# Row sums on TensorE for five attention units: four matmuls of 128 queries in place of sixteen of 32

## The chip, the cores and the metric

The kernel runs on one core of a Trainium2 chip. The metric is the device time of one execution in microseconds. The kernel before took 599.05 us (median of 3 runs, 598.12 to 600.31).

## The reference: what is computed

Chunked attention, and behind it a feed-forward block with a rational activation:

```python
for c in range(nc):                       # 24 chunks of 32 queries, per batch (4) and head (8)
    q_c = q[:, :, c_start:c_end]
    k_full = np.concatenate([mem_k, k_ctx], axis=2)   # 8 + up to 56 keys
    v_full = np.concatenate([mem_v, v_ctx], axis=2)
    scores = scale * np.matmul(q_c, k_full.transpose(0, 1, 3, 2))
    a = np.exp(scores - np.max(scores, axis=-1, keepdims=True))
    a = a / (np.sum(a, axis=-1, keepdims=True) + 1e-09)
    out[:, :, c_start:c_end] = np.matmul(a, v_full)
...
h = x @ w_in                              # x: 3072 x 512, w_in: 512 x 2048
P = a[0] + a[1] * h + a[2] * h2 + a[3] * h3
Q = 1.0 + np.abs(b[0]) * np.abs(h) + np.abs(b[1]) * h2
return (P / (Q + 1e-06)) @ w_out          # w_out: 2048 x 512
```

The weights w_in and w_out come as 64-bit floats and are turned into pairs of 32-bit ones on the chip.

## The kernel before, in words

The 3,072 tokens are six blocks of 512. A block's attention is worked in four units (i, p), one for each pair of heads: i is the block, p the pair. A unit has 16 chunks of 32 queries, and 64 keys for each of the two heads.

An early unit (i of 0 or 1) goes through these steps, each a function named here with its lines:

- att_scores (354): 16 matmuls of 32 queries each, which fill a PSUM tile of 128 x 512; places (268) puts four chunks at the four quarters of the 128 partitions, with a tile position for each.
- att_max, att_less (364, 371) on VectorE, att_exp (394) on ScalarE, and for a sequence's ends memsets on GpSimd (absent, 381).
- att_turn (404): four transposes of 128 x 128 into a PSUM tile ep; att_keep (414): ScalarE copies it to the SBUF tile eT. There the 128 partitions are the keys of both heads, and the 512 columns are the queries, chunk after chunk.
- att_values (421): 16 matmuls, each with the 32 columns of eT of one chunk as the weights and that chunk's values (128 x 128) as the moving side (line 428). For the five units in SUMS_PE (line 36: (0,0), (0,2), (1,0), (1,1), (1,2)) it then adds 16 matmuls with the same weights against a matrix "ones" of two columns, one for each head (line 434). They write the row sums into the first 8 columns of ep, which is free by then.
- att_more (330) reads the sums from ep on VectorE (line 334) and att_over (340) inverts them. For the other early units att_sums (319) takes the sums on VectorE instead (line 324).
- att_norm (437) scales the values, att_back (446) transposes back, att_hi and att_lo (456, 463) split the result into two parts for the feed-forward block.

The feed-forward block: g1 (480, matmuls at 489) makes h for 128 of the 2,048 features, a chain of steps on ScalarE, VectorE and GpSimd (554 to 614; chain_mend at 602 is the last but two) makes the activation, and g2 (491, matmuls at 504) adds its product with w_out. Each product is three matmuls of 128 x 128 weights and 512 columns. 96 such rounds run over the six blocks.

Order: up to the 31st round the order is written out by hand in SEQ (line 50), a list of tokens that is worked through once (740); each engine keeps the program's order (pin, 141). A lower-case "d" is att_values, "D" is att_more, "G" is att_over, "n" att_norm, "b" att_scores, "m" and "M" att_max and att_less, "x" att_exp, "c" att_turn, "k" att_keep, "e" att_back; "f" and "g" are g1, "o" is g2, "W" is a warm-up transpose (663), "P" a small matmul that spreads six parameters over the partitions (732). Around the first unit it reads "... d00 D00 b03 v01 w x02 M01 q10 G00 n00 x01 m03 W c02 c01 M03 e00 A k02 B d02 z01 D02 ... W W d01 ...". The PSUM tiles of the early units come from pa (260), which goes round four rooms: the values' tile of (0,2) is the room of the scores of (0,3), and the values' tile of (0,1) is the room of ep of (0,2), where its sums lie.

Of the kernel before, what the change touches and what calls it, by code (L numbers as in the profile page):

```python
# [19 lines left out]
CHUNK = 32  # L20
# [69 lines left out]
def attn_moe(ctx, tc, qk, vm, w, ab, out, seq):  # L90
    nc = tc.nc
    P = 128
# [5 lines left out]
    NC, NG = TB // CHUNK, TB // P  # L98
# [30 lines left out]
    ones = const.tile([P, 2], F32, name="ones")  # L129
# [11 lines left out]
    def pin(ins):  # L141
        if pinned[0]:
            tc.keep_in_program_order(ins)
# [116 lines left out]
    def pa(i):  # L260
        turn[0] = (turn[0] + 1) % 4
        if early[0]:
            if turn[0] == 3:
                return ps_r.tile([P, 512], F32, name="pa", tag="cr")
            return ps_o.tile([P, DM], F32, name="pa", tag=f"o{turn[0]}")
        return ps_a.tile([P, 512], F32, name="pa", tag="pa")

    def places(i):
        return [(g, j, 4 * g + j if i < BLOCKWISE else NG * j + g) for g in range(NG) for j in range(4)]
# [40 lines left out]
    def pair_values(i, p):  # L310
        u = unit[i, p]
        ov = u["o"] = two_banks("o", D)
        for g, j, c in places(i):
            for h in range(2):
                pin(nc.tensor.matmul(ov[j * CHUNK:(j + 1) * CHUNK, h, g],  # L315
                                     lhsT=u["eT"][h * KEYS:(h + 1) * KEYS, c * CHUNK:(c + 1) * CHUNK], rhs=u["v"][c][h],
                                     start=True, stop=True, tile_position=(h * KEYS, j * CHUNK)))
# [103 lines left out]
    def att_values(i, p):  # L421
        if i >= BLOCKWISE:
            return pair_values(i, p)
        u = unit[i, p]
        o = u["o"] = pa(i)
        ov = o.rearrange("x (g h d) -> x g h d", g=NG, h=2)
        for g, j, c in places(i):
            pin(nc.tensor.matmul(ov[j * CHUNK:(j + 1) * CHUNK, g],  # L428
                                 lhsT=u["eT"][:, c * CHUNK:(c + 1) * CHUNK], rhs=u["v"][c],
                                 start=True, stop=True, tile_position=(0, j * CHUNK)))  # L430
        if (i, p) in SUMS_PE:
            sv = u["ep"][:, :2 * NG].rearrange("x (g h) -> x g h", h=2)
            for g, j, c in places(i):
                pin(nc.tensor.matmul(sv[j * CHUNK:(j + 1) * CHUNK, g], lhsT=u["eT"][:, c * CHUNK:(c + 1) * CHUNK], rhs=ones,  # L434
                                     start=True, stop=True, tile_position=(0, j * CHUNK)))

    def att_norm(i, p):
        if i >= BLOCKWISE:
# [182 lines left out]

    att = {}
    pieces = dict(z=att_sums, D=att_more, G=att_over, b=att_scores, m=att_max, M=att_less, x=att_exp, c=att_turn, k=att_keep, d=att_values, n=att_norm, e=att_back, h=att_hi, l=att_lo)

    def plan(n, kind, i, p):
# [218 lines left out]
```

## Time and profile before

| | |
|---|---|
| median of 3 runs | 599.05 us (598.12 to 600.31) |
| the profiled execution | 598.73 us |
| its span, first to last instruction | 596.9 us |
| mean granted TensorE clock | 1.000 |
| matmul records on TensorE | 5,111, and as many loads of weights |
| busy: TensorE, VectorE, GpSimd, ScalarE | 98%, 78%, 68%, 67% |

PE is TensorE's matmuls and PEld its loads of weights, DVE is VectorE, ACT ScalarE, POOL GpSimd, SP the queue that issues the DMAs. L434 is line 434 of the kernel. An entry "128*32 128x2" of PE stands for weights of 128 rows and 32 columns and a moving side of 2 columns. Matmuls are pipelined, so their records overlap and a line's busy time is less than its count times the mean. "issue" is time in which an engine waited for nothing that the profile shows.

### The profile page before, as it was taken

The page shows a single profiled execution, that of the slowest core. Times are in us where ns is not written, and L with a number is a line of the kernel's source. Part 1 is how long each engine was busy: PE and PEld are TensorE (multiplying, and loading weights), DVE is VectorE, ACT ScalarE, POOL GpSimd, SP SyncE. Part 2 cuts the span into 40 slices and gives each one's busy share as a digit, 9 for nine tenths or more (in the row PEclk, how much of TensorE's full clock was granted, in tenths as well). Part 3 has the DMA queues.
Part 4 walks back from the last instruction along what each step waited for, and adds up shares of the span by engine and source line. Part 5 has one row for each costly group of instructions (what it writes and reads, how often), then busy time and mean ns, then how long its engine had stood idle before and what let it go on. Part 6 is the DMA issues. An engine that isn't in the chain of part 4 may idle for free.

```text
span 596.9 us, 13088 instructions
## 1 busy us (share of the span) xinstructions
PE 586.8 (98%) x5111; PEld 478.4 (80%) x5111; DVE 464.9 (78%) x762; ACT 401.9 (67%) x665; POOL 406.4 (68%) x376
## 2 busy tenths in 40 slices
PE   7899999999999999999999999999999999999997
PEld 6677888888787878878888888888888888888886
DVE  5899999898797759888877778787787766666673
ACT  4699999898667655656566666565765656755673
POOL 5468998798546766576677576766667677667682
PEclk9999999999999999999999999999999999999999
DMA  8965346230345344332331422312510100100001
GB/s 304 406 206 213 146 177 212 72 128 13 124 131 165 98 151 127 94 111 72 99 87 50 154 43 87 94 36 81 178 36 1 37 10 9 71 1 1 0 1 70
DMA packets 34591, 61.14 MB, mean 102 GB/s; under 512 B 4066, under 2 KB 20706, under 8 KB 34146
## 3 DMA queue, kind: packets, MB, share of 16 engines
q1 hardware_dynamic: 34386, 60.18, 30.6%
q8 instruction: 40, 0.66, 0.5%
q14 instruction: 21, 0.17, 0.1%
q10 hardware_dynamic: 144, 0.13, 0.1%
HBM read 44.56 MB, written 7.34 MB: 87 GB/s over the span
## 4 chain that ended last, share of the span: by engine, by line
PE 95%; DVE 2%; ACT 1%; DMA 1%; issue 0%; SPq 0%; POOL 0%; DVEq 0%
PE h L489 44%; PE o L504 43%; PE pairs L315 2%; PE pairs L293 2%; PE pa L428 1%; PE pa L361 1%; DMA qk<-in_qk_dram 1%; PE pa L412 1%; PE pa L454 0%; DVE e L379 0%; PE pa L434 0%; ACT e L396 0%; DVE ct L602 0%; ACT eT L419 0%; PE warm L663 0%
## 5 line engine op out<-in xcount | busy, mean ns | idle before, releaser
L489 PE MATMUL h<-x_hi,w_hl 128*128 128x512 f32 x768 | 240.3, 394 | 0.4 <-DVE ct L602 0.3
L504 PE MATMUL o<-w_hl,ghi 128*128 128x512 f32 x768 | 236.8, 390 | 0.0
L566 POOL TENSOR_TENSOR cy<-cy,ha 128x512 f32<-128x512 f32 x96 | 124.6, 1298 | 140.4 <-ACT cy L562 135.8
L504 PEld LDWEIGHTS o<-w_hl,ghi 128*128 128x128 f32 x768 | 143.9, 188 | 29.8 <-ACT v_main L546 0.2
L489 PEld LDWEIGHTS h<-x_hi,w_hl 128*128 128x128 f32 x768 | 141.7, 188 | 32.4 <-DVE ct L602 1.1
L489 PE MATMUL h<-x_lo,w_hl 128*128 128x512 f32 x384 | 150.0, 391 | 0.2 <-POOL x_lo L467 0.2
L504 PE MATMUL o<-w_hl,glo 128*128 128x512 f32 x384 | 150.0, 391 | 0.0
L614 POOL TENSOR_TENSOR glo<-ct,ghi 128x512 fp32r<-128x512 f32 x95 | 122.9, 1294 | 9.1 <-ACT ghi L609 3.2
L594 DVE SCALAR_TENSOR_TENSOR ct<-ct,par,h 128x512 f32<-128x512 f32 x82 | 61.2, 746 | 56.2 <-ACT h L590 55.5
L575 DVE TENSOR_TENSOR ct<-ct,h 128x512 f32<-128x512 f32 x96 | 65.6, 684 | 39.4 <-ACT ct L571 37.8
L586 ACT ACTIVATE h<-cy 128x512 f32<-128x512 f32 x82 | 49.1, 599 | 69.5 <-DVE ct L579 56.1
L557 ACT ACTIVATE ha<-h 128x512 f32<-128x512 f32 x96 | 57.4, 598 | 54.4 <-PE h L489 54.3
L607 POOL TENSOR_TENSOR ghi<-ct,zero 128x512 fp32r<-128x512 f32 x81 | 84.2, 1040 | 2.5 <-PE o L504 1.2
L504 PEld LDWEIGHTS o<-w_hl,glo 128*128 128x128 f32 x384 | 72.1, 188 | 16.8 <-POOL glo L614 1.6
L489 PEld LDWEIGHTS h<-x_lo,w_hl 128*128 128x128 f32 x384 | 72.1, 188 | 16.1 <-POOL x_lo L467 0.6
L562 ACT ACTIVATE cy<-ha,bab 128x512 f32<-128x512 f32 x96 | 78.4, 817 | 2.6
L571 ACT ACTIVATE ct<-h,par 128x512 f32<-128x512 f32 x96 | 73.6, 766 | 5.6 <-PE h L489 5.5
L579 DVE SCALAR_TENSOR_TENSOR ct<-ct,par,h 128x512 f32<-128x512 f32 x96 | 71.6, 746 | 3.0
L602 DVE SCALAR_TENSOR_TENSOR ct<-h,ct 128x512 f32<-128x512 f32 x82 | 56.5, 689 | 2.6
L598 DVE SCALAR_TENSOR_TENSOR h<-cy,h 128x512 f32<-128x512 f32 x82 | 56.5, 689 | 0.0
L590 ACT ACTIVATE h<-h 128x512 f32<-128x512 f32 x82 | 47.7, 582 | 2.6
L204 POOL TENSOR_TENSOR w_hl<-w_raw,w_hl 128x512 fp32r<-128x512 f32 x32 | 42.0, 1318 | 6.4 <-ACT w_hl L199 5.7
(80 smaller groups left out, 461.9 us busy)
## 6 DMA issues: line engine op xcount, KB each, us to landing
w_raw<-in_w_dram SPq DMA_DIRECT2D x26, 512.0 KB, 5.9
qk_pairs<-in_qk_dram SPq DMA_DIRECT2D x16, 576.0 KB, 4.2
v_main<-in_vm_dram SPq DMA_DIRECT2D x16, 512.0 KB, 5.1
out_dram<-v_main SPq DMA_DIRECT2D x23, 256.0 KB, 2.3
qk<-in_qk_dram SPq DMA_DIRECT2D x16, 288.0 KB, 5.8
eT<-blocks SPq DMA_DIRECT2D x64, 64.0 KB, 2.1
xf<-blocks SPq DMA_DIRECT2D x64, 64.0 KB, 2.1
v_main<-in_vm_dram SPq DMA_DIRECT2D x12, 256.0 KB, 6.4
```

The source lines that it names most:

```text
L489: pin(nc.tensor.matmul(h, lhsT=wt[:, cols], rhs=xt[i][:, ct, :], start=ct == m == 0, stop=ct == NCT - 1 and m == 2))
L504: ins = nc.tensor.matmul(o, lhsT=gt[:, cols], rhs=wt, start=begin and m == 0, stop=end and m == 2)
L557: pin(nc.scalar.activation(c["ha"], c["h"], AF.Abs))
L562: pin(nc.scalar.activation(c["y"], c["ha"], AF.Identity, scale=B1, bias=B0))
L566: pin(nc.gpsimd.tensor_tensor(c["y"], c["y"], c.pop("ha"), op=ALU.mult))
L571: pin(nc.scalar.activation(c["t"], c["h"], AF.Identity, scale=A3, bias=A2))
L575: pin(nc.vector.tensor_tensor(t, t, h, op=ALU.mult))
L579: pin(nc.vector.scalar_tensor_tensor(t, t, A1, h, op0=ALU.add, op1=ALU.mult))
L594: pin(nc.vector.scalar_tensor_tensor(t, t, A0, r, op0=ALU.add, op1=ALU.mult))
L598: pin(nc.vector.scalar_tensor_tensor(r, yy, QC, r, op0=ALU.add, op1=ALU.mult))
L607: pin(nc.gpsimd.tensor_tensor(ghi, chain[z]["t"], zero.broadcast_to([P, TB]), op=ALU.add))
L614: pin(engine.tensor_tensor(glo, chain.pop(z)["t"], gh[z].bitcast(F32), op=ALU.subtract))
```

## The change

The loop over the 16 places becomes a loop over the four groups of 128 queries; a group's four chunks lie next to each other in eT, and their sums go to the same places in ep as before.

```diff
         if (i, p) in SUMS_PE:
             sv = u["ep"][:, :2 * NG].rearrange("x (g h) -> x g h", h=2)
-            for g, j, c in places(i):
-                pin(nc.tensor.matmul(sv[j * CHUNK:(j + 1) * CHUNK, g], lhsT=u["eT"][:, c * CHUNK:(c + 1) * CHUNK], rhs=ones,
-                                     start=True, stop=True, tile_position=(0, j * CHUNK)))
+            for g in range(NG):
+                pin(nc.tensor.matmul(sv[:, g], lhsT=u["eT"][:, g * P:(g + 1) * P], rhs=ones, start=True, stop=True))
```

## Rows read from the trace of the kernel before

**Rows 1.** The page: busy time by engine, DMA packets of kind instruction

```profile
PE 586.8 (98%) x5111; PEld 478.4 (80%) x5111; DVE 464.9 (78%) x762; ACT 401.9 (67%) x665; POOL 406.4 (68%) x376
...
q8 instruction: 40, 0.66, 0.5%
```

**Rows 2.** The chain that ended last, 12 to 60 us: start, length, what

```profile
14.23 0.35 PE pa L434 x29
...
14.69 0.06 DVE rinv L334
...
16.34 1.13 issue
...
36.55 0.17 DVE rinv L334
36.72 0.61 DVE ct L602
...
37.37 3.00 PE h L489 x12
...
43.98 0.29 PE pa L434 x29
```

**Rows 3.** Busy time (instructions) in stretches: PE, PEld, DVE, ACT, POOL, clock, DMA, GB/s

```profile
16.00:18.00 2.00, 0.80 (x8) 0.70 (x7) 1.87 (x4) 1.19 (x3) 1.37 (x2) 1.00 1.04 419
...
60.00:100.00 40.00, 40.00 (x209) 32.78 (x207) 37.87 (x61) 37.62 (x64) 37.15 (x33) 1.00 0.47 169
...
400.00:590.00 190.00, 190.00 (x1261) 156.46 (x1260) 135.05 (x207) 119.25 (x190) 128.84 (x110) 1.00 0.11 34
```

**Rows 4.** Line 434 alone: count, duration min/median/max in ns, first and last start

```profile
L434 PEld LDWEIGHTS pa<-ones,eT x160: 106/113/113, 14.0 to 44.1; 128*32 128x32 f32 x160
L434 PE MATMUL pa<-ones,eT x160: 167/171/190, 14.1 to 44.1; 128*32 128x2 f32 x160
```

**Rows 5.** TensorE's loads in order of time: start, from first start to last end

```profile
12.79 0.20 PEld L663 LDWEIGHTS warm<-ident 128*128 128x128 f32 x2 [0.20 <-issue]
...
13.95 0.47 PEld L434 LDWEIGHTS pa<-ones,eT 128*32 128x32 f32 x32
...
22.22 0.29 PEld L732 LDWEIGHTS warm<-par,x_lo 1*128 1x128 f32 x2 [0.17 <-issue]
22.53 0.30 PEld L489 LDWEIGHTS h<-x_hi,w_hl 128*128 128x128 f32 x2
```

**Rows 6.** TensorE's matmuls in order of time, the same columns

```profile
11.78 1.08 PE L361 MATMUL pa<-qk 128*32 128x128 f32 x32
...
18.43 1.08 PE L428 MATMUL pa<-v_first,eT 128*32 128x128 f32 x32
19.33 0.45 PE L434 MATMUL pa<-ones,eT 128*32 128x2 f32 x32
...
35.11 1.08 PE L428 MATMUL pa<-v_main,eT 128*32 128x128 f32 x32
36.01 0.45 PE L434 MATMUL pa<-ones,eT 128*32 128x2 f32 x32
36.40 0.66 PE L412 MATMUL pa<-ident,e 128*128 128x128 f32 x4
...
42.08 0.60 PE L454 MATMUL pa<-ident,xt 128*128 128x128 f32 x4
```

**Rows 7.** Groups of loads and matmuls by form: count, busy us, mean ns of one

```profile
L489 PEld LDWEIGHTS h<-x_hi,w_hl 128*128 128x128 f32 x768 | 141.7, 188 | 32.4 <-DVE ct L602 1.1 <-issue 0.9 <-POOL w_hl L204 0.2
...
L412 PEld LDWEIGHTS pa<-ident,e 128*128 128x128 f32 x32 | 3.6, 140 | 2.8 <-POOL e L392 1.5 <-issue 1.2
...
L732 PEld LDWEIGHTS warm<-par,x_lo 1*128 1x128 f32 x2 | 0.3, 182 | 0.2 <-issue 0.2
```

**Rows 8.** VectorE in order of time, 13 to 21.5 us

```profile
17.05 0.69 DVE L379 TENSOR_TENSOR e<-pa,mx 128x512 f32<-128x512 f32 x1
...
19.92 0.17 DVE L334 TENSOR_SCALAR rinv<-pa 128x8 f32<-128x8 f32 x1 [0.98 <-PE pa L434]
```

## The prediction

> **What bounds the kernel now.** I began with the page: TensorE's matmuls are busy for 98% of the span and no other engine is above 78% [rows 1]. Busy time alone could hide short gaps, since matmuls overlap in the records, so I read the chain of waits next. Over the stretch from 12 to 60 us it runs mostly over TensorE, and all five blocks of sums lie on it (the first at 14.23 with 0.35 us, the last at 43.98 with 0.29) [rows 2]. Twice the chain leaves TensorE right behind a block of sums, for VectorE: at 14.69 and at 36.55 VectorE waits for the sums before it can go on (line 334), and TensorE's next work waits for VectorE. So the sums are on the path that sets the end, in a stretch that is otherwise a ladder of PE, DVE and ACT steps. From 60 us on TensorE has no idle time: 40.00 of 40.00 us, and 190.00 of 190.00 near the end, at a granted clock of 1.00 [rows 3]. What the sums lose or gain by 45 us is therefore carried to the end, unless something before that takes it up.
>
> **What the change removes.** A matmul on f32 is recorded as two passes, each with a load of weights, so a unit's sixteen matmuls are 32 loads and 32 passes (160 of each over five units) [rows 4]. The four new ones are 8 loads and 8 passes. The columns loaded are the same: 32 times 32 or 8 times 128, 1,024 in all. What is given up is that the four quarters of the array are loaded side by side. Today 32 loads take 0.47 us from the first start to the last end; less one load of 0.11 that is 0.36, or 0.012 us from one start to the next [rows 4, 5]. Passes move two columns and take 0.17 us from start to end, but they overlap. Hence a block of sums ends only 0.27 us behind the values' block in front of it: 36.01 + 0.45 = 36.46 against 35.11 + 1.08 = 36.19, and 19.33 + 0.45 = 19.78 against 18.43 + 1.08 = 19.51 [rows 6].
>
> **What it adds.** Nowhere does this kernel load 128 columns for so small an f32 matmul except at line 732 (1 row, 6 columns moved), and there the second of two loads starts 0.29 - 0.18 = 0.11 us behind the first; two loads in front of the h matmuls, of 128 rows, do the same (0.30 - 0.19 = 0.11) [rows 5, 7]. I take 0.107. The nearest row that is cheaper is the transposes' load: 0.20 - 0.14 = 0.06 us from the first to the second of two warm-ups [rows 5, 7]. It belongs to a transpose and not to a product, so I keep it as the lower bound, and 0.12 (0.107 and the rounding of these rows) as the upper one.
>
> The timing of one block, with E the end of the values' block: a full-width load behind a block of quarters starts at about E - 0.07 (the scores end at 11.78 + 1.08 = 12.86, the warm-up's load starts at 12.79) [rows 5, 6]. The eighth load starts 7 x 0.107 = 0.75 later, at E + 0.68; its pass begins 0 to 0.11 behind it and takes 0.17. The sums then end at E + 0.85 to E + 0.96, not E + 0.27: 0.58 to 0.69 later, and I take **0.63**. That is the price where VectorE waits for them. Where TensorE simply goes on, a ninth load (for the next block) starts at E + 0.79, its first matmul up to 0.11 later, and four transposes without a change of width in front take 0.60 (the block at 42.08) [rows 6], so they end at E + 1.39 to 1.50. Now they end at 36.40 + 0.66 = 37.06, or E + 0.87. That is 0.52 to 0.63 later, and I take **0.57**: the step from quarter to full width that stands behind the sums today moves in front of them, so it isn't paid twice.
>
> Unit by unit:
> - Unit (0,0), sums at 14.1 [rows 4]: **about 0**. VectorE's step at line 334 comes 0.63 later, and with it all that is queued behind it on VectorE up to the subtraction that starts at 17.05 and ends at 17.74 [rows 8]. The next values' block needs that subtraction (its output tile is the one that the subtraction reads) and starts now at 18.43. It waits today for TensorE, which lost 1.13 us in "issue" at 16.34 [rows 2, 6]. 17.74 + 0.63 = 18.37 is just before 18.43, so the idle time covers it. If that cover is gone the unit costs 0.6. Here the next block is in quarters, so two changes of width are added; both lie under the same cover.
> - Unit (0,2), sums at 19.33: **0.63**. VectorE stands idle for 0.98 us until they end (its step at 19.92), and the next values' block writes the tile that this step reads [rows 8].
> - Unit (1,0), sums at 36.01: **0.63**. VectorE waits, and behind line 334 stands the last step of a chain (line 602), for which TensorE's h at 37.37 waits [rows 2].
> - Units (1,1) and (1,2), whose sums come last, up to 44.1 [rows 4]: TensorE goes straight on, **0.57** each.
>
> The sum is 0.63 + 0.63 + 0.57 + 0.57 = **2.40 us**. No queue is reordered and no DMA is added; on TensorE about 240 recorded loads and passes of 10,222 go. The profiled execution took 598.73 us (its span is 596.9, with 1.8 around it), so it would take 601.1. It lies 0.3 below the median of 599.05; by the median I forecast 601.4, that is 0.40% slower.
>
> **A rule against this.** The 32 passes start 0.45 - 0.17 = 0.28 us apart from first to last, 9 ns each [rows 4, 6], so no fixed price per matmul is seen here that would repay fewer of them. The Trainium skill says otherwise (TensorEngine Tiling (Array Packing), Instruction Overhead): each matmul has about 60 cycles of overhead, and a dimension that is already small shouldn't be tiled. By it, at 2.4 GHz, 24 passes fewer of 25 ns would save 0.6 us a unit, an estimate of 3 us in all and a time of 596. The row at 19.33 doesn't agree: 32 passes at that price would need 0.8 us, and the block takes 0.45.
>
> **Rivals.**
> - *Cheap loads* (not slower). If a load of 128 columns costs 0.057 us as the transposes' does, the eighth starts at E + 0.33 and the sums end at about E + 0.55, 0.28 later; TensorE's next block ends 0.15 later. The sum is 2 x 0.28 + 2 x 0.15 = 0.9 us, 599.9: no change that can be measured. For it: those loads are 128 x 128 and f32 too. Against: both rows of true products show 0.11. It decides from about 0.088 us a load, where the sum falls under 1.8.
> - *Taken up behind 44 us.* VectorE is busy for 37.87 of 40 us between 60 and 100 us [rows 3]. If it sets the pace there, the last two units' delay on TensorE is lost in it: 1.26 us are left, 600.3. Against: TensorE shows no idle time there.
> - *Code comes late.* The 1.13 us of "issue" fall where all DMA engines are busy (1.04) [rows 2, 3]. Packets of kind "instruction" number 40 with 0.66 MB [rows 1], 256 instructions each if TensorE's 10,222 are what they carry, so that wait may be for a block of code. With 48 recorded instructions fewer ahead of it the block is wanted about one unit's work later. I expect it to have landed by then; if instead the wait comes back inside the next unit, its 1.13 us join the path: 2.4 + 1.1 = 3.5 us, 602.6.
> - *A price per pass.* If a wide pass costs the same 9 ns as a narrow one, 24 fewer save 0.2 us a unit on four units, 0.9 us: 598.2.
>
> **How the numbers follow.** I give my sum 0.55, cheap loads 0.17, code 0.12, the delay taken up 0.08, a price per pass 0.05, and 0.03 to what I don't see. A measurement of this kernel can tell about 0.3%, 1.8 us, from no change. My sum is 0.6 us above that, and single runs differ by 2.2 us, so a fifth of its chance goes to "same". Slower: 0.55 x 0.8 + 0.12 + 0.01 = 0.57. Faster by 1.8 us needs more than any row offers: 0.03. Same: 0.40. The range runs from just under the cheap loads (599.3) to between the code's case and my upper bound with no cover for unit (0,0): 2.6 + 0.7 = 3.3, with the runs' spread 603.0.
>
> **What would show it.** In the changed kernel's profile line 434's loads should number 40 with about 0.18 us each, and a unit's 8 should take some 0.93 us from the first start to the last end (7 x 0.107 + 0.18). VectorE should wait longer at line 334, in the second and third unit by about 0.6 us, and at all in the fourth. The h matmuls behind the last sums (44.1) should start about 2.4 us later, and the tail from there should be as long as before. The "issue" gap at 16.34 should be gone or smaller with nothing won by it. I am wrong if the loads follow each other in 0.06 us, if the shift at 44 us shrinks before the end, or if a new gap of a microsecond stands somewhere on TensorE before 30 us.

## The result, and the profile after

The changed kernel takes **603.06 us** (median of 5 runs, 602.50 to 603.48) against 599.05: a ratio of **1.0061**, 95% interval 1.0043 to 1.0079. It is slower, as forecast, but by 4.0 us and not by 2.4; the value lies 0.06 us above the end of the range. A second measurement (the experiment e2 below) gave 602.57 and 1.0053 (1.0036 to 1.0070).

The profiled execution took 603.48 us, its span is 601.6. Lines after 434 are one less than before (h is 488, o 503). The page first, lines that answer to [rows 1]:

```profile
PE 591.3 (98%) x4991; PEld 481.3 (80%) x4991; DVE 465.0 (77%) x762; ACT 401.9 (67%) x665; POOL 406.2 (68%) x376
...
q8 instruction: 39, 0.64, 0.4%
```

TensorE has 120 passes and 120 loads fewer, and one packet of instructions less. Its matmuls are busy for 4.5 us more; VectorE, ScalarE and GpSimd change by 0.2 at most. Next TensorE's loads in order of time, with start and time from first start to last end, beside [rows 5]:

```profile
15.06 0.97 PEld L434 LDWEIGHTS pa<-ones,eT 128*128 128x128 f32 x8 [0.20 <-issue]
```

Eight loads take 0.97 us where 32 took 0.47. Line 434 alone, beside [rows 4]:

```profile
L434 PEld LDWEIGHTS pa<-ones,eT x40: 186/192/192, 15.1 to 48.3; 128*128 128x128 f32 x40
L434 PE MATMUL pa<-ones,eT x40: 251/251/272, 15.1 to 48.3; 128*128 128x2 f32 x40
```

A load of 128 columns here lasts 0.19, so one starts (0.97 - 0.19) / 7 = 0.111 us behind the other, and a pass lasts 0.25 where a narrow one lasts 0.17. The matmuls, same columns, beside [rows 6]:

```profile
14.05 1.08 PE L428 MATMUL pa<-v_main,eT 128*32 128x128 f32 x32
15.06 1.05 PE L434 MATMUL pa<-ones,eT 128*128 128x2 f32 x8
...
19.38 1.08 PE L428 MATMUL pa<-v_first,eT 128*32 128x128 f32 x32 [0.37 <-ACT eT L419]
...
26.72 0.84 PE L428 MATMUL pa<-v_first,eT 128*32 128x128 f32 x18 [0.15 <-ACT eT L419]
27.89 0.64 PE L428 MATMUL pa<-v_first,eT 128*32 128x128 f32 x14 [0.32 <-issue]
28.45 0.73 PE L488 MATMUL h<-x_hi,w_hl 128*128 128x512 f32 x2
...
44.28 1.05 PE L434 MATMUL pa<-ones,eT 128*128 128x2 f32 x8
45.20 0.63 PE L412 MATMUL pa<-ident,e 128*128 128x128 f32 x4
...
48.43 0.48 PE L488 MATMUL h<-x_hi,w_hl 128*128 128x512 f32 x1
...
246.34 0.79 PE L293 MATMUL pairs<-qk_pairs 64*32 64x64 f32 x59
247.53 0.30 PE L293 MATMUL pairs<-qk_pairs 64*32 64x64 f32 x3 [0.40 <-issue]
```

A block of sums now ends 15.06 + 1.05 - (14.05 + 1.08) = 0.98 us behind its values, before 0.27. Two rows show waits that the sum of the prediction didn't hold. At 27.89 TensorE stands still in the middle of 32 equal passes of unit (0,3), whose sums the change doesn't touch, and at 247.53 it does so in the middle of 62 passes, some 200 us behind the last changed instruction. Nothing of the program ends these waits; "issue" is all that the profile names. In the trace of before both blocks run through: the values of (0,3) stand as one row of 32 at 25.09, and these are its rows at the second place:

```profile
242.13 0.82 PE L293 MATMUL pairs<-qk_pairs 64*32 64x64 f32 x62
242.88 0.73 PE L489 MATMUL h<-x_hi,w_hl 128*128 128x512 f32 x2
```

Pieces of the chain that ended last in the changed kernel, 12 to 60 us (start, length, what), beside [rows 2]:

```profile
15.13 1.00 PE pa L434 x8
...
16.22 0.06 DVE rinv L334
...
18.67 0.59 ACT eT L419
...
20.45 0.98 PE pa L434 x8
...
27.56 0.32 issue
...
38.49 1.00 PE pa L434 x8
39.51 0.17 DVE rinv L334
39.67 0.61 DVE ct L601
40.33 3.01 PE h L488 x12
...
44.35 0.98 PE pa L434 x8
...
47.59 0.98 PE pa L434 x8
48.57 2.88 PE h L488 x12
```

The gap of 1.13 us at 16.34 [rows 2] is gone, and the path there now runs over DVE and ACT (ACT's copy at 18.67), as worked out for a unit whose cover is just used up. The sums are on the path five times. What VectorE waited for up to 62 us (us in total, times, longest):

```profile
DVE rinv L334 <- PE pa L434: 3.8, 4, 1.1
```

Before, this line read 1.7 us, 3 times, 1.0 at most. The tail is as it was; busy time in two stretches, columns as in [rows 3]:

```profile
60.00:100.00 40.00, 40.00 (x207) 32.50 (x207) 37.92 (x62) 37.90 (x65) 38.38 (x34) 1.00 0.48 176
400.00:590.00 190.00, 190.00 (x1261) 156.44 (x1260) 135.99 (x211) 121.13 (x194) 130.34 (x112) 1.00 0.12 36
```

**Where the time went.** I followed the same instruction through both traces and noted by how much it starts later. In the first pair of traces the shift grows like this:

- Ahead of any changed instruction: 0.49 at the first scores, 0.89 at the scores of 11.78 [rows 6], which now start at 12.67.
- Unit (0,0): 0.06, so covered: its successor goes from 18.43 [rows 6] to 19.38.
- Unit (0,2): 0.69. Unit (1,0): 0.66 (h from 37.37 [rows 2] to 40.33). Units (1,1) and (1,2): 0.63 and 0.62 (values from 42.91 to 46.50, h from 44.20 to 48.43).
- The standstill in the values of (0,3): 0.72 (h behind them from 26.10 to 28.45, where the shift had been 1.64). The one at 247.53: 0.6 (62 passes and the next h 1.42 us apart, before 242.88 - 242.13 = 0.75; 0.07 of it is made up right behind).
- At the end: 601.6 - 596.9 = 4.7.

The five units come to 0.06 + 0.69 + 0.66 + 0.63 + 0.62 = 2.66 us, close to the forecast. Two standstills add 1.3 and the start 0.9, and both had to be explained.

### The profile page after: what moved, and what is told of

Same layout as the page of the kernel before. It is cut to its first block, busy times and chain, and to the rows that moved or that the text cites. A ratio compares the mean times of both kernels' runs of the same rounds, so it can differ in the third digit from the quotient of the medians.

```text
span 601.6 us, 12848 instructions
## 1 busy us (share of the span) xinstructions
PE 591.3 (98%) x4991; PEld 481.3 (80%) x4991; DVE 465.0 (77%) x762; ACT 401.9 (67%) x665; POOL 406.2 (68%) x376
## 4 chain that ended last, share of the span: by engine, by line
PE 95%; DVE 2%; ACT 1%; DMA 1%; issue 0%; SPq 0%; POOL 0%; DVEq 0%
PE h L488 44%; PE o L503 43%; PE pairs L315 2%; PE pairs L293 2%; PE pa L428 1%; PE pa L361 1%; PE pa L434 1%; DMA qk<-in_qk_dram 1%; PE pa L453 1%; PE pa L412 1%; ACT eT L419 0%; DVE e L379 0%; DVE ct L601 0%; ACT e L396 0%; PE warm L662 0%
```

## The experiments

My theory after this reading: wide loads cost 2.7 us; the standstills are waits for blocks of TensorE's code, and the change brings them onto the path because its 240 fewer instructions move the ends of the blocks; the later start is chance. The rivals: the start belongs to the change; the standstills come and go by chance, whatever the count of instructions; and wide loads cost less or more than the trace suggests.

**e1 and e2: each kernel again, unchanged.** There is no edit. Of e1 (before):

> The kernel before, unchanged, profiled once more, to see what the start-up does from one execution to the next. In the first profile of the changed kernel the first scores (line 361) start at 7.17 us instead of 6.68, and the warm-up behind them 0.89 us later than before, all ahead of the first changed instruction. Theory A (the start-up is chance: when the first load lands and when TensorE's clock is let up): the time stays at 599 +- 0.7 us, but the first scores may start anywhere from 6.6 to 7.3 us. Theory B (the 0.89 us belong to the change, by the program's place or size): 6.68 again, to 0.1 us.

Of e2 (after):

> The changed kernel once more. Theory A (start-up is chance): first scores anywhere from 6.6 to 7.3 us, time 603 +- 0.7. Theory B: 7.17 again. On both: 8 loads of a unit's sums take 0.97 us; TensorE stands still for some 0.5 us inside the values of unit (0,3), behind 18 of their 32 passes, which is behind 705 loads, passes and semaphore records of TensorE, and again 16 x 256 records later, near 247 us, if those two gaps are waits for a block of 256 instructions; if they were chance they need not come back.

e1 gave 598.81, ratio 0.9994 (0.9982 to 1.0007); e2 602.57, as above. The first scores' rows in e1 and in e2, 5 to 8 us:

```profile
6.71 1.67 PE L361 MATMUL pa<-qk 128*32 128x128 f32 x25 [2.02 <-DMA qk<-in_qk_dram]
```

```profile
6.63 1.08 PE L361 MATMUL pa<-qk 128*32 128x128 f32 x32 [1.94 <-DMA qk<-in_qk_dram]
```

The changed kernel started at 7.17 in its first trace and starts at 6.63 here, before the unchanged one: the 0.9 us at the start belongs to that execution, not to the change. Both standstills came back. The first one in e2 (order of time on TensorE, 24 to 29 us):

```profile
25.66 0.84 PE L428 MATMUL pa<-v_first,eT 128*32 128x128 f32 x18 [0.15 <-ACT eT L419]
27.09 0.64 PE L428 MATMUL pa<-v_first,eT 128*32 128x128 f32 x14 [0.60 <-issue]
```

It is the same pass, behind 18 of 32, though 1 us earlier in time, and it costs more (shift 1.0). At the second place 0.4 is lost. The second trace gives 0.1 + 0.69 + 0.66 + 0.69 + 0.62 = 2.8 for the sums, 1.0 + 0.4 for the standstills and -0.2 at the start, 4.0 together. Its span is 600.6 - 596.9 = 3.7 longer than before, and the medians differ by 3.5. The unchanged kernel isn't free of such waits either: in e1's trace TensorE stands still for 0.39 us ("issue") at 24.17, in the middle of scores.

**The count.** I counted what TensorE's queue holds ahead of each standstill: passes, loads, and the semaphore and drain records of its sequencer. The stretches that hold them, of before (16.34 in [rows 2]) and of after (columns as in [rows 3]):

```profile
0.00:17.46 17.46, 12.18 (x219) 10.49 (x220) 10.60 (x19) 7.67 (x11) 9.52 (x23) 1.00 0.89 319
```

```profile
0.00:27.50 27.50, 22.21 (x344) 18.37 (x344) 17.76 (x35) 13.53 (x24) 11.17 (x26) 1.00 0.93 354
0.00:247.40 247.40, 240.92 (x2244) 194.56 (x2245) 205.70 (x348) 184.19 (x314) 173.04 (x170) 1.00 0.46 161
```

Before: 219 + 220 passes and loads and 10 others are 449. After: 344 + 344 + 17 = 705, and 2,244 + 2,245 + 56 = 4,545. These are 193 + 256, 193 + 2 x 256 and 193 + 17 x 256. A packet of kind "instruction" carries 0.64 MB / 39 = 16 KB, and some 10,000 records in 39 packets are 256 each. The Trainium skill has the same number (Runtime: NRT & Kernel Launch, Instruction fetch mechanics): an engine's code is refilled in blocks of 256 instructions, and crossing a block's end is "mostly hidden". The trace agrees on 256 and on most ends; it disagrees where the passes are short (at 247 us) or the DMA engines busy (a share of 0.93 up to 27.5 us), by 0.25 to 1.9 us a time here.

**e9: before, with its count shifted.** The sums are those of before; eight warm-up matmuls more at the very start, behind which TensorE waits for data anyway, add 16 records. Since -240 and +16 differ by 256, a block must end at the same pass at 247 us as in the changed kernel.

```diff
-WARM = 14
+WARM = 22
```

> The kernel before with 22 warm-up transposes at the start instead of 14, which fit into the wait for the first load (4.7 to 6.7 us): 16 recorded loads and passes more ahead of everything. By the count of blocks (every 256 recorded instructions from the 449th on) the end of a block then falls on the same pass of line 293 near 242 us as in the changed kernel, where that one stood still. Theory A (the waits are for blocks of code, and where they fall is set by the count alone): a gap of 0.4 to 0.6 us there, in a kernel whose sums are unchanged, none of it in the two profiles of the kernel before; 599.4. Rival (the gap belongs to the changed sums): none. Beside it the clock may come up earlier at the start, which would win up to 0.9 us: 598.2 to 599.6 in all.

Measured: 601.52 (600.06 to 603.36) beside 598.95, ratio 1.0038 (1.0024 to 1.0051). TensorE in order of time, 13 to 19 and 244 to 249 us:

```profile
14.27 1.07 PE L361 MATMUL pa<-qk 128*32 128x128 f32 x30
17.25 0.41 PE L361 MATMUL pa<-qk 128*32 128x128 f32 x2 [1.91 <-issue]
...
245.89 0.79 PE L293 MATMUL pairs<-qk_pairs 64*32 64x64 f32 x59
247.11 0.30 PE L293 MATMUL pairs<-qk_pairs 64*32 64x64 f32 x3 [0.43 <-issue]
```

The standstill stands behind pass 59 of 62, to the instruction where the count puts it, with not one sum changed. That settles that the second wait comes from the count. The time I had put too low. Up to record 449 nothing is lost (these scores start at 14.27, before at 14.50), so the added warm-ups cost nothing by themselves. Then the first block's end fell into scores, where TensorE stood still for 1.9 us; 1.2 of them the kernel before loses too, in its gap at 16.34. I had not looked at the next end, record 705, which costs another standstill of 0.70 at 26.31, and behind the first one the clock fell (last section). The profiled execution is the slowest of the eleven, so these sizes are not those of the median. By the medians a kernel that computes the same with the same sums is 0.4% slower with 16 records more.

**e3 and e4: the change in three units and in two.** e3 changes the units of block 1, e4 those of block 0 (the edit against the kernel before; "..." stands for lines left out):

```diff
-            for g, j, c in places(i):
+            if i == 1:
+                for g in range(NG):
...
+            else:
+                for g, j, c in places(i):
```

> The change in the three units (1,0), (1,1), (1,2) alone. Theory A (loads in a row, 0.11 us each, all on the path): 0.66 + 0.62 + 0.64 = 1.9 us more than before, 601.0, as the three steps measured in the changed kernel's profile. The gap of 1.1 us at about 16.4 is where it was in the kernel before (nothing ahead of it has moved), none stands in the values of (0,3). Rival (each unit pays a fifth of the whole 4.0 us): 2.4 us, 601.5. Rival (the delay is taken up behind 44 us): under 0.7 us.

e3 gave 601.14, ratio 1.0031 (1.0019 to 1.0043). Its trace has the steps 0.65, 0.68 and 0.62, 1.95 in sum for a difference of 2.0 us. The gap of 16.34, which I expected to stay, has shrunk to 0.18 us, since its code had landed by 15.49 here. Its next block's end (record 705) falls into scores at 24.67 ahead of values that wait for ACT in any case. These three units' loss goes through to the end whole.

e4 has the same edit with `if i == 0:`.

> The change in the two units (0,0) and (0,2) alone. Theory A: 0.1 for (0,0), whose delay lies under the wait that VectorE's queue sets, 0.7 for (0,2), and a gap of about 0.6 us in the values of (0,3), since TensorE's 256-instruction blocks end there as in the whole change: 1.4 us in all, 600.5. Without the gap 599.9. Rival (unit (0,0) is not covered): 0.7 us more than that.

e4 gave 600.74, ratio 1.0023 (1.0009 to 1.0037). The steps are 0.14 and 0.69. Its profiled execution has no gap in the values of (0,3), although the count there is that of the changed kernel, but it has one far behind:

```profile
429.56 0.39 PE L493 MATMUL h<-x_lo,w_hl 128*128 128x512 f32 x1
430.46 0.72 PE L493 MATMUL h<-x_hi,w_hl 128*128 128x512 f32 x2 [0.52 <-issue]
```

That is behind record 8,385, or 193 + 32 x 256: an end of a block again, and it costs 430.46 - 429.56 = 0.90 where passes here otherwise follow after 0.23: 0.67 us, which with the two steps makes 1.50 of the 1.6. So the count says where a wait can fall, not that it falls. e3 and e4 add up: 2.0 + 1.6 = 3.6 us against 3.5 and 4.0 for the whole.

**e10: the change in the first unit alone** (against the kernel before).

```diff
-            for g, j, c in places(i):
+            if (i, p) == (0, 0):
+                for g in range(NG):
...
+            else:
+                for g, j, c in places(i):
```

> The change in unit (0,0) alone. Theory A (its delay lies under waits that are there anyway): the values of (0,2) start within 0.15 us of where they start in the profile of before, counted from the first scores' end, and the time is that of before, 599.1 to 599.3. Rival (not covered): 0.7 us more, 599.8.

599.05 beside 598.95, ratio 0.9993 (0.9981 to 1.0004): the first unit's loss is covered. The small step itself can't be read here, since the profiled execution (600.93) has a long start of its own, with 1.93 us for the scores that take 1.08 in [rows 6].

**e5: the changed kernel with fewer warm-ups.**

```diff
-w q00 b00 m00 q02 A q01 M00 b02 v00 x00 B C q03 m02 w Y v02 c00 W W b01 m01 M02 H k00 W W d00 D00 b03 v01 w x02 M01
-q10 G00 n00 x01 m03 W c02 c01 M03 e00 A k02 B d02 z01 D02 k01 h00 v03 L x03 A D01 G02 n02 G01 W W d01 w w e02 z03 c03
+w q00 b00 m00 q02 A q01 M00 b02 v00 x00 B C q03 m02 w Y v02 c00 W W b01 m01 M02 H k00 d00 D00 b03 v01 w x02 M01
+q10 G00 n00 x01 m03 W c02 c01 M03 e00 A k02 B d02 z01 D02 k01 h00 v03 L x03 A D01 G02 n02 G01 d01 w w e02 z03 c03
```

> The changed kernel without four warm-up transposes (two ahead of the values of (0,0), two ahead of those of (0,1)): 8 recorded loads and passes fewer ahead of the two gaps. Theory A (the gaps are waits for blocks of 256 instructions, counted from the program's start): the gap in the values of (0,3) comes again behind the 705th record, which is now 4 passes further on (22 and 10 passes, not 18 and 14), and the gap near 247 us moves out of the short passes of line 293 into the h matmuls, where it is under 0.3 us or gone: 0 to 0.4 us less than the changed kernel. Rival (the gaps hang on these instructions, by a semaphore or a bank): they stay behind the 18th pass and inside line 293. The warm-ups themselves fill waits: no time is won or lost by them.

602.21 beside 599.08, ratio 1.0048 (1.0031 to 1.0066). In time it can't be told from the changed kernel. In the trace the late standstill left the short passes for the h matmuls, as the count has it:

```profile
246.53 0.82 PE L293 MATMUL pairs<-qk_pairs 64*32 64x64 f32 x62
247.28 0.98 PE L488 MATMUL h<-x_hi,w_hl 128*128 128x512 f32 x2
```

It costs 0.98 - 0.73 = 0.25 us there. In the values of (0,3) no gap shows, though the block still ends inside them, four passes on, as expected; this is the second such case after e4. Not every "issue" wait is at an end: without the warm-ups TensorE waits for 0.38 us ahead of the values of (0,1), 48 records behind one.

**When the code lands.** The traces also hold the start and the landing of every packet of kind "instruction". On the queue q8 there are 40 packets before and 39 after, and behind record 193 there are 39 and 38 ends of blocks, so I put the n-th packet to the n-th end (times in us):

| run, record at the end | packet starts | lands | next record starts | behind the landing | matmuls idle |
|---|---|---|---|---|---|
| before, 449 | 15.01 | 16.02 | 17.47 | 1.45 | 1.20 |
| e9, 449 | 15.07 | 16.04 | 17.25 | 1.22 | 1.91 |
| after, 449 | 15.10 | 16.13 | 19.73 | 3.61 | none |
| before, 705 | 21.32 | 22.38 | 23.88 | 1.50 | none |
| after, 705 | 25.49 | 26.56 | 27.88 | 1.32 | 0.32 |
| e2, 705 | 24.77 | 25.75 | 27.09 | 1.35 | 0.60 |
| e4, 705 | 23.26 | 24.36 | 27.18 | 2.81 | none |
| e5, 705 | 24.12 | 25.07 | 28.11 | 3.04 | none |
| after, 4,545 | 244.89 | 246.23 | 247.53 | 1.30 | 0.40 |
| e9, 4,801 | 244.53 | 245.84 | 247.11 | 1.27 | 0.43 |
| e4, 8,385 | 428.08 | 429.01 | 430.46 | 1.45 | 0.52 |

The twelve traces of this case have 462 such ends. At none does the next record start sooner than 1.22 us behind its packet's landing. At 18 it starts 1.22 to 1.50 us behind it, and at 15 of these TensorE's matmuls are idle (0.08 to 1.91 us, twice with a wait for GpSimd beside it); at the other 444 it starts 1.71 us or more behind it, and no "issue" wait of the matmuls stands there. So the standstills are waits for code, and (0,3) has none in e4 and e5 because the packet had landed over 2.8 us ahead. Two things make a packet late here. Up to 28 us, where the DMA engines are busy, the packet for record 705 starts 3.2 to 6.7 us after the block ahead of that end has begun; for the ends behind record 961 it starts 0.7 us before that in the median. Near 245 us the DMA engines are idle (a share of 0.02 from 242 to 246), but in the changed kernel the packet starts only as the block ahead of the end begins (record 4,289 at 244.91), and that block is used up before the packet's 1.3 us and the 1.3 behind them have passed.

**e6: half the width.** Eight matmuls of 64 queries, two side by side:

```diff
             for g in range(NG):
-                pin(nc.tensor.matmul(sv[:, g], lhsT=u["eT"][:, g * P:(g + 1) * P], rhs=ones, start=True, stop=True))
+                for j in range(2):
+                    pin(nc.tensor.matmul(sv[j * 2 * CHUNK:(j + 1) * 2 * CHUNK, g], lhsT=u["eT"][:, g * P + j * 2 * CHUNK:g * P + (j + 1) * 2 * CHUNK],
+                                         rhs=ones, start=True, stop=True, tile_position=(0, j * 2 * CHUNK)))
```

> One size changed: eight matmuls of 64 queries a unit, two side by side, in place of four of 128. Theory A (a load's price is its columns, and loads at different column positions go side by side): 16 loads of 0.055 in pairs, so the eighth pair starts 0.40 behind the first and the sums' block ends 0.35 to 0.45 us earlier than at full width; over four units 1.4 to 1.8 us less than the changed kernel without its code waits, 600.0 to 600.8. Rival (no two loads side by side at this width): 16 loads take 0.85 in a row, time as the changed kernel. The code's blocks fall elsewhere again, up to 0.7 us.

599.71, ratio 1.0006 (0.9996 to 1.0016), and in its trace steps of 0.36, 0.30, 0.27 and 0.29, or 1.2 us, in the four units behind (0,0). The time is below what I expected and shows only 0.6, in part because (0,0) wins 0.3 here: the gap at 16.34 is gone, no other wait takes its place, and a shift of 0.15 at the scores of 11.78 is -0.18 at the values of (0,2). The loads:

```profile
14.32 0.55 PEld L435 LDWEIGHTS pa<-ones,eT 128*64 128x64 f32 x16 [0.20 <-issue]
```

Less one load of 0.137 that is (0.55 - 0.137) / 15 = 0.028 us from start to start, 0.055 a pair. The same 1,024 columns take 0.47 us in quarters, 0.55 in halves and 0.97 in one piece: the loss follows how many loads lie beside each other, and falls while the count of passes rises.

**e7: the sums taken twice.** The second round writes the same values again.

```diff
-            for g in range(NG):
+            for g in list(range(NG)) * 2:
```

> The changed kernel with each unit's four sums matmuls issued twice, which write the same numbers again: 8 more loads a unit. Theory A (0.111 us a load, all on the path from the second unit on): 0.89 us a unit in four units, 3.6 us, and most of 0.89 in (0,0) now that its cover of 0.65 is used up: 4.0 to 4.5 us over the changed kernel, 606.6 to 607.4. Rival (the sums are partly off the path): less, down to 603.5 where only VectorE's two waits count.

608.16 (607.12 to 611.45) beside 599.08, ratio 1.0154 (1.0129 to 1.0179). The loads do what was expected:

```profile
14.21 1.86 PEld L434 LDWEIGHTS pa<-ones,eT 128*128 128x128 f32 x16 [0.20 <-issue]
```

The second eight add 1.86 - 0.97 = 0.89 us, 0.111 each. The time is above what I expected, and the windows show why (columns as in [rows 3]):

```profile
24.00:26.00 2.00, 2.00 (x16) 1.57 (x8) 0.95 (x2) 0.50 (x2) 0.00 (x0) 0.50 0.99 397
...
44.00:46.00 2.00, 2.00 (x6) 1.57 (x5) 2.00 (x5) 1.27 (x3) 1.77 (x4) 0.50 0.81 263
```

Behind doubled sums the granted clock fell to 0.50, the level of 1.2 GHz, twice, for the two microseconds shown and some time around them. In both traces of the changed kernel it stays at 1.00 from the first sums on. So the doubled run bounds a load's price by its trace, not by its time.

**e8: narrow sums right behind each group's values.** Sixteen narrow matmuls as before, in another order, to see if the old form leaves something to win (the new lines, which stand inside the loop of the values):

```diff
+            if (i, p) in SUMS_PE and j == 3:
+                for k in range(4):
+                    m = c - 3 + k
+                    pin(nc.tensor.matmul(sv[k * CHUNK:(k + 1) * CHUNK, g], lhsT=u["eT"][:, m * CHUNK:(m + 1) * CHUNK], rhs=ones,
+                                         start=True, stop=True, tile_position=(0, k * CHUNK)))
```

> The kernel before with its sixteen narrow sums kept, but a group's four sums put right behind its four values matmuls. In the profile of before a group's values take 0.21 us (8 passes of 128 columns, four side by side at 0.107), and loads of 32 columns go on beside them. Theory A: the sums' loads hide beside the values' passes and the block of sums' 0.27 us shrinks to the passes that remain, 0.1: 0.1 to 0.2 us less a unit in four units, 598.3 to 598.7; not to be told from 599.1. Rival (a load waits for the pass that uses the same columns): no change, or 0.1 us a unit more, 599.6.

599.13, ratio 0.9996 (0.9986 to 1.0005): no change. From a unit's values to the next scores it takes 14.49 - 13.33 = 1.16 us where e1 has 14.53 - 13.20 = 1.33, and none of it is seen in the time. No version tried beats the kernel before.

## Why the prediction was right and wrong, point by point

- **Direction: right.** The sums were on the path, wide loads are slower, and what they lost by 48 us stayed lost: e3's three units cost 1.95 us in the trace and 2.0 in the time.
- **The price of a load: right, a little low.** 0.111 against the 0.107 taken from two pairs of loads [rows 5, 7]. e7 gives the same for eight more, so they follow each other in a row, and no second price stands beside it.
- **Unit by unit.** (0,0) at nothing: right, at 0.06 and 0.1 in the two traces and no change in e10; the "issue" gap was its cover, as said. The other four come to 0.69, 0.66, 0.63 and 0.62 where 0.63, 0.63, 0.57 and 0.57 were taken. The mis-sized term is the end of the sums, E + 0.98 where I had E + 0.85 to 0.96: I gave the last pass the 0.17 us of a narrow one, and it takes 0.25. My sum was 2.40, the measured one 2.66 and 2.8.
- **The step that failed: one wait for code, where there is one at every block's end.** I had seen that the gap at 16.34 might be a wait for code and had the number, 256 to a packet, but treated it as a single event that either comes back or not, and the code's case as a rival of the sum with a chance of 0.12. "I expect it to have landed by then" was right for that block: in the changed kernel its packet is there 3.6 us ahead of record 449. The ends behind it I put at nothing without a reason. Every 256 records a wait can fall, and what the change moves is where: record 705 went out of covered ground (scores, behind which the values wait for ACT in any case) into the values of (0,3), which nothing covers, and another end, at 247 us, into 62 short passes. By e2 they add 1.0 + 0.4 us to 2.8. So loads and code are two terms of one sum. That the rival's figure of 602.6 comes near 602.57 and 603.06 is luck: it brought back the old wait of 1.13 us in the next unit, and what came were two waits for other blocks, in other places. The sign that I had named for being wrong, a new gap on TensorE before 30 us, is there at 27.89, with 0.7 us lost and not a microsecond (1.0 in e2).
- **Cheap loads** (0.057 each): refuted by 0.97 us for eight, and by e2, e3. **Taken up behind 44 us**: refuted by the shift, 48.43 - 44.20 = 4.23 us there and 246.34 - 242.13 = 4.21 at 242 us. **A price per pass**: refuted by e6, where twice the passes of the changed kernel cost half its loss. With it falls, for these passes, the rule of 60 cycles that I had weighed from the Trainium skill (TensorEngine Tiling (Array Packing), Instruction Overhead): 32 narrow passes took 0.45 us, 16 of half width 0.63, and 8 wide ones 1.05.
- **What stays open.** Why the early packets start late, and by how much more in one execution than in another: that they queue behind the data is argued from the DMA engines' share alone. What passes in the 1.2 to 1.5 us between a packet's landing and the first record isn't shown. The wide sums were not run with their count put back by 240 records; that they cost 2.7 us without the waits rests on the traces' steps and on e3. What sets the first load's landing between 6.63 and 7.17 us was not tried, nor another shift of before's count that might do better than before.

## What to carry to other kernels

Where small matmuls side by side in quarters of the array load their weights side by side too, as here, fewer and wider ones move the same columns through one place in a row, so count columns in series, not instructions. A change that adds or removes instructions also moves each later end of a code block: number the engine's records, mark the ends 256 apart, and look at which of them leave a wait of another kind and land in a run of short passes, and at how long ahead of each its packet lands. To tell the two effects apart, shift the count alone in a stretch where the engine is idle, as e9 did.

## What the runs showed of the hardware that I had not expected

- A standstill at the end of a block of 256 records costs 0.25 to 1.9 us here, and it fell behind record 193 + n x 256 in every case that I counted: 449 (before, e9), 705 (e1, after, e2, e3, e9), 4,545 (after, e2, e5), 4,801 (e9), 8,385 (e4). Most ends show nothing. TensorE never started on a block sooner than 1.22 us behind the landing of its code.
- A standstill may cost twice. After the 1.9 us in e9 TensorE's granted clock fell to 0.50 (windows of e9, columns as in [rows 3]):

```profile
18.00:20.00 2.00, 2.00 (x11) 2.00 (x11) 1.46 (x3) 0.80 (x2) 0.00 (x0) 0.50 0.97 371
```

- The same level follows doubled wide sums, in e7, where no long standstill went before: TensorE was busy for 1.90 of the 2 us from 22 to 24, in which the first fall begins, and for 1.64 of those from 42 to 44, at whose end the second does. Eight wide loads a block kept 1.00 in both traces of the changed kernel, sixteen didn't. What lowered the clock, in e7 or in e9, isn't shown.
